# Attention: the row maxima are turned by VectorE in four blocks, the sign sits in the keys' constant row

## The chip, the cores and the metric

One core of a Trainium2 chip runs the whole program. The time is the device time of one execution in microseconds (us), and the number reported is the median of several runs. The core has five engines that run side by side, each through its own queue of instructions in order: TensorE (PE in the profile, with its weight loads as PEld), VectorE (DVE), ScalarE (ACT), GpSimd (POOL) and SyncE (SP, which here only issues transfers). They meet through semaphores.

## The reference

Four layers work on one sequence of 2048 tokens with 512 channels, all in fp32. Layers A are linear attention with learned features; layers B split the sequence into 4 segments of 512 tokens, and each segment is attended with a softmax, beside a memory of the segments before it. Only layer B's softmax matters here:

```python
for s in range(N):                       # 4 segments, 32 heads of 16 channels
    qs, ks, vs = q[:, :, s], k[:, :, s], v[:, :, s]
    logits = jnp.einsum("bhqd,bhkd->bhqk", qs, ks) * scale + mask
    p = _softmax(logits, axis=-1)
    a_dot = jnp.einsum("bhqk,bhkd->bhqd", p, vs)
    ...
x = x + _A_ref(...); x = x + _B_ref(...); x = x + _A_ref(...); x = x + _B_ref(...)
```

A softmax needs the maximum of each row of logits, so that the exponentials stay in range.

## The kernel before

A layer B works in quarter-steps, called m in the code: 8 of them in a segment (4 groups of 8 heads, each in two halves of 4 heads), 32 in a layer, 64 in the run. A quarter-step has five steps (R = 5), numbered k; the loop in `steps` (L1449) goes through k and issues, in program order, what belongs to each step. A table (`FIRST`, `GAPS`, `LAST`, `FINAL`) tells which further work is issued at which step: "2.0 m0 max turn t1 fin ln" is the first step of quarter-step 2. The wrapper `Ordered` (L144) and `held` (L164) tie every engine's instructions to the order in which the program issues them, so nothing moves on its own.

Each quarter-step holds queries and keys of its heads in the tiles Q and K, on 128 partitions: two groups of 64 rows. Of each group, 63 rows hold high and low parts of the values, and constants; row 63 (and 127) holds a constant 1 in K and is free in Q.

- `maxima(m)` runs 9 steps ahead of the attention (`LEAD`). It multiplies 63 rows of Q and K on TensorE, tokens on partitions, into two PSUM banks (tags "mx" and "my", or "g" in two of the five steps), and VectorE adds the mask and takes the maximum of each row in one instruction (L1165). Its accumulator goes to one column of the tile mxs, 128 tokens x 16 columns, one column for each of 4 heads and 4 blocks of 128 queries. The profile shows these instructions as CUSTOM_DVE_ANT_0, each with a DVE_READ_ACCUMULATOR2_ANT that writes mxs.
- `put_maxima(m)` (the word "max" in the table) comes in the step of the last of them. The maxima lie along partitions and are needed along a row, so TensorE turns mxs into the bank "mx" (L180, a transpose against the identity), ScalarE copies it to the tile mt with the factor -1, and at the next step the ScalarE queue issues a transfer from mt into rows 63 and 127 of Q (the list `self.later`).
- `attend(m)` begins four steps later. It multiplies all 64 rows, so that row 63 adds the negative maximum (Q) times 1 (K) to each logit. ScalarE exponentiates (P<-lg in the profile), GpSimd zeroes what lies above the diagonal, and `weighted(m)` multiplies by the values (g<-P,v) one step after the last block.

In the step in which `put_maxima` runs, the program's order is: products of the attention and of the maxima, then transfers and parts put off from earlier steps, then the weighted sums of the quarter-step before, and then the words of the table. There "m0" to "m3" (the memory's update, tile mem) stand ahead of "max", and "turn" (ot or tmp, through oh and ol), "a" (reading the memory: g<-mem,tb and r) and "fin" (turning U, then r and wt or ot) behind it.

The constants come from the host: column 25 of bd is 1 at partitions 15 and 31, and `constants` (L211) spreads it to the tile `ones`, from which `start` (L994) fills the constant rows of K. The tile mxs is taken anew for each quarter-step (two buffers), and so is mt.

Of the kernel before, what the change touches and what calls it, by code (L numbers as in the profile page):

```python
# [7 lines left out]
F32 = mybir.dt.float32  # L8
F32R = mybir.dt.float32r
BF16 = mybir.dt.bfloat16  # L10
AF = mybir.ActivationFunctionType
# [7 lines left out]
P = 128  # L19
# [11 lines left out]
MT = 2  # L31
# [69 lines left out]
def interleave_kernel(ctx, tc, x_in, a_wqkv, a_wphi, a_wo, b_wq, b_wk, b_wv, b_wo, b_beta,  # L101
# [13 lines left out]
    def nm(s):  # L115
        uid[0] += 1
        return f"{s}_{uid[0]}"

    def T2(tag, bufs, dt=F32, shape=(P, 512)):
        return sp.tile(list(shape), dt, tag=tag, bufs=bufs, name=nm(tag))  # L120

    def PS(tag, bufs, shape=(P, 512)):
        return ps.tile(list(shape), F32, tag=tag, bufs=bufs, name=nm(tag))
# [38 lines left out]
    dve, act, pool, sync = [Ordered(e) for e in (nc.vector, nc.scalar, nc.gpsimd, nc.sync)]  # L162

    def held(i):  # L164

        if last[0] is not None:
            behind(i, last[0])
        last[0] = i
        return i
# [3 lines left out]
    def mm(*a, **k):  # L173
        n = a[0].free_size()
        work[0] += n / 2.26 if k["rhs"].dtype == F32R else (n * 2 / 2.4 + 25 if "tile_position" in k else 2 * max(112, n * 2 / 2.4))
        return held(nc.tensor.matmul(*a, **k))  # L176

    def tp(*a):
        work[0] += 108
        return held(nc.tensor.transpose(*a))  # L180

    def dma(out, in_):
        sync.dma_start(out=out.bitcast(F32), in_=in_.bitcast(F32))

    ident = cp.tile([P, P], F32, name="ident")
    bd = cp.tile([P, 27], F32, name="bd")
# [793 lines left out]
    class LayerB:  # L980
# [6 lines left out]
        def start(self):  # L987
            mem = sp.tile([P, NC, 10 * VW], F32, tag="acc", bufs=1, name=nm("mem"))
            self.acc, self.kn = mem[:, :, 0 : 2 * VW], mem[:, :, 2 * VW :]
            self.sets = []  # L990
            for b in range(NSET):
                Q, K = [T2("e8", 2 * NSET, F32R, (P, 4, 512)) for _ in range(2)]
                self.sets.append((Q, K))
                for t, rows in ((Q, mask[0:32, 0:P]), (K, ones)):  # L994
                    dma(t[3:P:4].rearrange("p a t -> p (a t)"), rows.unsqueeze(1).broadcast_to([32, 16, P]))
                    yield
# [150 lines left out]
        def maxima(self, m):  # L1147


            s, c, hf = m // 8, m % 8 // 2, m % 2  # L1150
            Q, K = [t[:, 2 * hf : 2 * hf + 2, :] for t in self.st[s, c]["set"]]
            mx = T2("mxs", 2, shape=(P, 16))

            def prod(pb, r, i, at, w):
                for e in range(2):
                    q, k = Q[64 * e : 64 * e + 63, r, :], K[64 * e : 64 * e + 63, r, :]
                    mm(pb[e][:, at : at + w], lhsT=q[:, i * P : (i + 1) * P], rhs=k[:, 0:w],
                       start=True, stop=True, tile_position=(64 * e, 0))

            def top(pb, e, r, i, at):  # L1160
                n = (i + 1) * P
                col = (e * 2 + r) * 4 + i
                pl = pb[e][:, at : at + n]
                with tc.high_priority():
                    dve.tensor_tensor_reduce(  # L1165
                        out=pl, in0=pl, in1=mask[:, 512 - n : 512], scale=1.0, scalar=-3.0e38,
                        op0=ADD, op1=MAX, accum_out=mx[:, col : col + 1])

            for what in ([(0, 0, 0), (0, 2, P)], [(0, 3, 0)], [(1, 0, 0), (1, 2, P)],
                         [(0, 1, 0), (1, 1, 256)], [(1, 3, 0)]):  # L1170
                if self.k % R in SPARE if self.k >= 0 else self.k % 2:
                    pb = [PS("g", G) for _ in range(2)]
                else:
                    pb = [PS(t, 1) for t in ("mx", "my")]
                for r, i, at in what:
                    prod(pb, r, i, at, max(256, (i + 1) * P))
                for r, i, at in what:
                    for e in range(2):
                        top(pb, e, r, i, at)
                self.mx[m] = mx  # L1180
                yield

        def put_maxima(self, m):
            s, c, hf = m // 8, m % 8 // 2, m % 2
            Q = self.st[s, c]["set"][0][:, 2 * hf : 2 * hf + 2, :]
            pt = PS("mx", 1)
            tp(pt[0:16, 0:P], self.mx.pop(m), ident)
            mt = T2("mt", MT, F32R, shape=(16, P))
            act.activation(mt, pt[0:16, 0:P], AF.Copy, scale=-1.0)
            self.later.append(lambda: act.dma_start(out=Q[63:P:64].bitcast(F32), in_=mt.bitcast(F32)))  # L1190

        def attend(self, m):

# [366 lines left out]
```

## Time and profile before

| | us |
|---|---|
| median of 3 runs | 1357.32 |
| lowest and highest run | 1356.66, 1358.54 |
| span of the profiled execution | 1355.4 |
| attention of the first layer B, span's start at 0 | some 262 to 672 |
| attention of the second layer B | some 930 to 1330 |
| TensorE and VectorE busy in 850 to 990 (layer A's second pass, mostly) | 137.10 and 109.65 of 140.00 |

The profiled execution's span, from the first to the last instruction of the program, is its own time as far as the profile tells it. In a group of the page the busy time and the mean ns of one instruction stand behind the count, and then the idle time of the engine before them with what ended it. A row of the timeline gives start and duration, the engine, line and operation, the tiles written and read, the count of merged instructions, and in square brackets the idle time ahead of it with its releaser. A row of the waits gives who waited for whom, us in total, how many times and the longest. Most instructions show L154, the line of the wrapper, or L176 and L180, the helpers for matmuls and transposes, so the tiles' names tell them apart. The DMA of mt shows as e<-mt, as Q is a tile with the tag e8.

### The profile page before, as it was taken

Reading aid. Unit: us, or ns where it says so; the run is one execution under the profiler, and the core shown is the slowest. Engines: PE = TensorE matmul, PEld = TensorE weight load, DVE = VectorE, ACT = ScalarE, POOL = GpSimd, SP = SyncE. Lnnn points to the kernel's source line nnn. Section 1 sums busy time; section 2 is a strip of 40 time slices with the busy share of each in tenths; the row PEclk is TensorE's granted clock in tenths of the full one; section 3 lists DMA queues with packets and bytes.
Section 4 is the critical chain, followed back from the end, with each engine's and each line's share of the span. In section 5 each row is a group of like instructions: output and inputs, shape, how many; then the busy total and the mean of one; then the engine's idle time right before and its main releaser. Section 6 shows DMA issues by size and latency. Waiting matters only on the chain.

```text
span 1355.4 us, 36817 instructions
## 1 busy us (share of the span) xinstructions
PE 1315.4 (97%) x14056; PEld 1032.6 (76%) x14056; DVE 1039.5 (77%) x3256; ACT 808.6 (60%) x1205; POOL 695.8 (51%) x1060
## 2 busy tenths in 40 slices
PE   7999989999999999999999998999999999999998
PEld 6888868777777777877768886886777777777765
DVE  4766778777888888888667677787778879878883
ACT  5556345547677677677544433453667866766754
POOL 1668666326447557345324356553355656554442
PEclk9999999999999999999999999999999999999999
DMA  6398447535654545546250103755556554554431
GB/s 205 102 336 276 151 135 234 170 100 138 174 166 131 158 118 134 154 119 184 90 184 33 64 33 126 241 164 134 138 159 175 145 160 105 140 136 103 118 96 63
DMA packets 134401, 196.27 MB, mean 145 GB/s; under 512 B 15441, under 2 KB 61649, under 8 KB 133457
## 3 DMA queue, kind: packets, MB, share of 16 engines
q1 hardware_dynamic: 132256, 193.27, 48.9%
q8 instruction: 112, 1.84, 0.5%
q10 hardware_dynamic: 1968, 0.64, 0.2%
q14 instruction: 65, 0.52, 0.1%
HBM read 101.05 MB, written 39.85 MB: 104 GB/s over the span
## 4 chain that ended last, share of the span: by engine, by line
PE 74%; DVE 10%; ACT 5%; issue 4%; POOL 3%; DMA 3%; SPq 1%; ACTq 0%; DVEq 0%; POOLq 0%
PE g L176 56%; PE lg L176 6%; PE g L180 6%; PE mx L176 3%; ACT P L154 3%; POOL P L154 2%; DVE g L154 2%; PE lg L180 2%; SPq L154 1%; POOL tb L154 1%; PE my L176 1%; DMA x<-x 1%; DVE es L154 1%; PE mx L180 1%; DVE my L154 1%
## 5 line engine op out<-in xcount | busy, mean ns | idle before, releaser
L154 ACT ACTIVATE P<-lg 128x1024 f32<-128x1024 f32 x316 | 325.4, 1030 | 167.1 <-PE lg L176 92.5
L154 POOL TENSOR_SCALAR_AFFINE_SELECT P<-P 128x256 f32<-128x256 f32 (+1 forms) x448 | 193.4, 446 | 283.7 <-ACT P L154 279.1
L154 DVE CUSTOM_DVE_ANT_0 g<-g,mask 128x256 f32<-128x256 f32 (+3 forms) x392 | 191.3, 542 | 8.9 <-PE g L176 8.5
L176 PE MATMUL g<-hh,wqk 64*128 64x512 f32 (+1 forms) x960 | 187.3, 392 | 0.5 <-DMA wqk<-wqk 0.4
L176 PE MATMUL g<-w,oh 64*128 64x512 f32 (+2 forms) x880 | 178.9, 385 | 0.6 <-DVE ol L154 0.6
L154 DVE CUSTOM_DVE_ANT_0 mx<-mx,mask 128x512 f32<-128x512 f32 (+2 forms) x316 | 157.4, 498 | 21.5 <-PE my L176 13.7
L154 DVE CUSTOM_DVE_ANT_0 my<-my,mask 128x512 f32<-128x512 f32 (+2 forms) x316 | 163.3, 517 | 0.0
L176 PE MATMUL g<-P,v 128*32 128x128 f32 (+3 forms) x2064 | 151.6, 433 | 3.6 <-DVE mxs L154 2.5
L176 PE MATMUL lg<-e,e 64*128 64x512 f32 (+1 forms) x1010 | 152.0, 339 | 3.1 <-ACT P L154 3.1
L176 PE MATMUL g<-w,hh 64*128 64x512 f32 (+1 forms) x672 | 143.4, 395 | 2.0 <-ACT w L154 1.3
L154 DVE DVE_READ_ACCUMULATOR2_ANT mxs<- 128x1 f32 x1024 | 142.7, 139 | 0.0
L176 PEld LDWEIGHTS g<-P,v 128*32 128x32 f32 x2064 | 61.5, 109 | 87.3 <-issue 59.2
L176 PEld LDWEIGHTS lg<-e,e 64*128 64x128 f32 x1010 | 102.1, 185 | 32.3 <-issue 11.3
L176 PEld LDWEIGHTS g<-w,oh 64*128 64x128 f32 (+1 forms) x880 | 108.3, 186 | 15.6 <-issue 1.5
L176 PEld LDWEIGHTS g<-hh,wqk 64*128 64x128 f32 (+1 forms) x960 | 106.9, 185 | 16.4 <-PE my L176 1.2
L176 PE MATMUL g<-w,ol 64*128 64x512 f32 (+2 forms) x440 | 116.9, 378 | 0.5 <-DVE ol L154 0.5
L154 POOL TENSOR_SCALAR tb<-tb 128x512 f32<-128x512 f32 x72 | 109.0, 1526 | 16.0 <-ACT tb L154 16.0
L176 PE MATMUL g<-hl,wqk 64*128 64x512 f32 (+1 forms) x480 | 106.8, 390 | 0.2
L154 ACT COPY tb<-g 128x512 f32<-128x512 f32 (+1 forms) x132 | 71.1, 576 | 43.5 <-PE g L176 41.7
L176 PEld LDWEIGHTS g<-w,hh 64*128 64x128 f32 (+1 forms) x672 | 84.4, 188 | 16.1 <-ACT w L154 1.6
L176 PE MATMUL g<-w,hl 64*128 64x512 f32 (+1 forms) x336 | 90.2, 393 | 0.0
L154 DVE TENSOR_REDUCE es<-P 128x64 f32<-128x1024 f32 x64 | 77.3, 1208 | 12.8 <-ACT P L154 12.8
(151 smaller groups left out, 2896.9 us busy)
## 6 DMA issues: line engine op xcount, KB each, us to landing
e<-ta SPq DMA_DIRECT2D x384, 128.0 KB
wqk<-wqk SPq DMA_DIRECT2D x128, 256.0 KB
x<-x SPq DMA_DIRECT2D x48, 256.0 KB
ot<-in SPq DMA_DIRECT2D x26, 256.0 KB
pq<-tb SPq DMA_DIRECT2D x24, 256.0 KB
tb<-pq SPq DMA_DIRECT2D x24, 256.0 KB
x<-xr SPq DMA_DIRECT2D x22, 256.0 KB
xr<-x SPq DMA_DIRECT2D x20, 256.0 KB
```

Of the source, the lines that this page charges most:

```text
L154: i = f(*a, **k)
L176: return held(nc.tensor.matmul(*a, **k))
L180: return held(nc.tensor.transpose(*a))
```

## The change

The tile of the maxima gets 32 columns instead of 16, and is no longer taken anew: `start` takes two for the layer, fills them with zeros once on GpSimd, and the quarter-steps use them in turn. `put_maxima` turns them on VectorE: four transposes of 32 x 32 elements, each from 32 partitions of mxs into 32 columns of mt, which now has 32 partitions. The first 16 rows of mt are what the transfer takes; the other 16 hold the turned zeros. TensorE's transpose, the use of bank "mx" for it and ScalarE's copy go away. The maxima stay positive and unrounded in Q, and the constant row of K is -1.

```diff
@@ start
             self.sets = []
+            self.tops = [T2("mxs", 2, shape=(P, 32)) for _ in range(2)]
+            for t in self.tops:
+                pool.memset(t, 0.0)
@@ maxima
-            mx = T2("mxs", 2, shape=(P, 16))
+            mx = self.tops[m % 2]
@@ put_maxima
-            pt = PS("mx", 1)
-            tp(pt[0:16, 0:P], self.mx.pop(m), ident)
-            mt = T2("mt", MT, F32R, shape=(16, P))
-            act.activation(mt, pt[0:16, 0:P], AF.Copy, scale=-1.0)
-            self.later.append(lambda: act.dma_start(out=Q[63:P:64].bitcast(F32), in_=mt.bitcast(F32)))
+            mt, mx = T2("mt", MT, shape=(32, P)), self.mx.pop(m)
+            for b in range(4):
+                dve.transpose(out=mt[:, 32 * b : 32 * b + 32], in_=mx[32 * b : 32 * b + 32, :])
+            self.later.append(lambda: act.dma_start(out=Q[63:P:64].bitcast(F32), in_=mt[0:16]))
@@ kernel
-    bd[[15, 31], 25] = 1.0
+    bd[[15, 31], 25] = -1.0
```

## The prediction

> **What bounds the kernel now.** I read the page first, then the busy time of each engine in the two attention stages (columns: stretch, then busy time and instructions of PE, PEld, DVE, ACT, POOL, then clock and DMA).
>
> ```profile
> span 1355.4 us, 36817 instructions
> ...
> PE 1315.4 (97%) x14056; PEld 1032.6 (76%) x14056; DVE 1039.5 (77%) x3256; ACT 808.6 (60%) x1205; POOL 695.8 (51%) x1060
> ...
> PE 74%; DVE 10%; ACT 5%; issue 4%; POOL 3%; DMA 3%; SPq 1%; ACTq 0%; DVEq 0%; POOLq 0%
> PE g L176 56%; PE lg L176 6%; PE g L180 6%; PE mx L176 3%; ACT P L154 3%; POOL P L154 2%; DVE g L154 2%; PE lg L180 2%; SPq L154 1%; POOL tb L154 1%; PE my L176 1%; DMA x<-x 1%; DVE es L154 1%; PE mx L180 1%; DVE my L154 1%
> ```
> ```profile
> 262.00:672.00 410.00, 404.53 (x4377) 313.77 (x4375) 336.97 (x1286) 277.02 (x402) 205.59 (x362) 1.00 0.52 141
> 930.00:1330.00 400.00, 391.70 (x4347) 301.38 (x4348) 327.11 (x1259) 266.17 (x385) 205.11 (x356) 1.00 0.49 131
> ```
> TensorE is busy 796 of the 810 us in which the 64 quarter-steps of attention (32 in each of two layers, some 12.7 us each) run, with the granted clock at 1.00. So time is gained here only by taking work or idle time from TensorE, and lost by making it wait. VectorE is the next in line: 664 of 810 us, 82%. ScalarE (67%) and GpSimd (51%) have room.
>
> **The change, part by part.** *Removed: 64 TensorE transposes and 64 ScalarE copies.* Two views by tile carry them (columns: count, then shortest/median/longest ns), with the accumulator reads that fill the maxima:
>
> ```profile
> L154 DVE DVE_READ_ACCUMULATOR2_ANT mxs<- x1024: 132/140/145, 262.0 to 1322.5; 128x1 f32 x171
> ...
> L180 PE MATMUL mx<-ident,mxs x64: 276/277/278, 280.8 to 1323.4; 128*16 128x128 f32 x64
> ```
> ```profile
> L154 ACT ACTIVATE mt<-mx x64: 245/249/267, 281.1 to 1324.1; 16x128 fp32r<-16x128 f32 x64
> ```
> 64 x 277 ns would be 17.7 us, but matmuls overlap. Two places of the timeline tell what one transpose really takes: the first has it between the weighted sums (g<-P,v) and the four turns of ot, the second has the same neighbours without it.
>
> ```profile
> 614.00 2.36 PE L176 MATMUL g<-P,v 128*32 128x512 f32 x32
> 616.29 0.28 PE L180 MATMUL mx<-ident,mxs 128*16 128x128 f32 x1
> 616.40 0.60 PE L180 MATMUL g<-ident,ot 128*128 128x128 f32 x4
> ...
> 677.92 2.36 PE L176 MATMUL g<-P,v 128*32 128x512 f32 x32
> 680.21 0.66 PE L180 MATMUL g<-ident,ot 128*128 128x128 f32 x4
> ```
> With it, the sums end at 616.36 and the turns at 617.00: 0.64 us. Without it, 680.28 to 680.87: 0.59 us. The transpose is worth only 0.05 to 0.06 us (I take 0.057), since whichever matmul follows the narrow 128*32 ones pays for the changeover. The chain of waits books 1% (some 13 us) on it, because it charges it with that changeover; I do not believe that share.
>
> In some places even that is lost, because TensorE then waits for something the change does not move:
>
> ```profile
> 604.18 0.28 PE L180 MATMUL mx<-ident,mxs 128*16 128x128 f32 x1
> 604.29 0.60 PE L180 MATMUL g<-ident,ot 128*128 128x128 f32 x4
> 605.06 0.66 PE L180 MATMUL g<-ident,U 128*128 128x128 f32 x4 [0.16 <-ACT U L154]
> ```
> ```profile
> PE g L176 <- DVE mxs L154: 3.5, 11, 0.5
> ...
> PE g L180 <- ACT U L154: 2.5, 7, 0.6
> ```
> U is made from the weighted sums, so it comes no earlier. I count 13 such places (6 of these 7 waits that follow a transpose, and 7 where the memory product next in line waits for a VectorE result). That leaves 49 x 0.057 = 2.8 us, with the first step of each layer counted apart.
>
> The first step of each layer is dearer: there the next products need bank mx, and wait for the copy out of it.
>
> ```profile
> 280.84 0.22 PE mx L180
> 281.06 0.02 issue
> 281.08 0.28 ACT mt L154
> 281.36 0.04 issue
> 281.40 0.50 PE mx L176
> ```
> This is the chain itself: 1.06 us from 280.84 to 281.90. With the transpose gone the products follow at once, for some 0.4 us (an estimate: their 0.50, partly under the matmul before): 0.65 us saved, twice, 1.3 us. The bank is then free since VectorE's last reading of it, so VectorE is late next there, not ScalarE.
>
> The copies were on ScalarE, off the chain but for these two; 16 us less there I cost at nothing, as ScalarE's next work mostly waits for TensorE.
>
> *Added: 256 transposes on VectorE.* The trace has none. Nearest rows, all of 32 columns or fewer:
>
> ```profile
> L154 DVE RECIPROCAL rr<-es 128x32 f32<-128x32 f32 x32 | 11.3, 353 | 1.4
> ...
> L154 DVE TENSOR_TENSOR rr<-rr,es 128x32 f32<-128x32 f32 x32 | 6.2, 192 | 1.1
> ...
> L154 DVE TENSOR_SCALAR eb<-eb 128x32 f32<-128x32 f32 x1 | 0.2, 169 | 0.0
> ```
> The accumulator read (139 ns) is the floor, the reciprocal (353 ns) the ceiling; the one with one input and plain arithmetic (169 ns) is nearest. Four in a row, with 0.1 us for the wait on the maxima just written: between 4 x (0.139 - 0.08) + 0.1 = 0.34 us, if each overlaps the one before by 0.08 us as VectorE's neighbours do below (464.23 + 0.69 against 464.84), and 4 x 0.353 + 0.1 = 1.5 us without overlap. I take 0.75 us, by the 169 ns row hardly overlapped (0.78 without any overlap): 48 us on VectorE in all, 664 becoming 712 of 810 us (88%).
>
> [...]
>
> What hides the group is a hole: VectorE has nothing to do while TensorE runs the weighted sums. The tightest kind (with the memory update, mem, ahead of it) and a wide one:
>
> ```profile
> 464.23 0.69 DVE L154 SCALAR_TENSOR_TENSOR tb<-tb,tb 128x512 f32<-128x512 f32 x1
> 464.84 0.18 DVE L154 TENSOR_TENSOR mem<-g,mem 128x34 f32<-128x34 f32 x1
> 465.44 0.17 DVE L154 TENSOR_SCALAR r<-g 128x16 f32<-128x16 f32 x1 [0.42 <-PE g L176]
> ```
> ```profile
> 603.26 0.14 DVE L154 DVE_READ_ACCUMULATOR2_ANT mxs<- 128x1 f32 x1
> ...
> 605.65 0.69 DVE L154 TENSOR_TENSOR ol<-g,oh 128x512 fp32r<-128x512 f32 x1 [2.25 <-ACT oh L154]
> ```
> Laid out for all 60 steps behind the first two of each layer, the hole at the new instructions' place is 0.41 to 0.46 us in 10 steps, 0.64 in one, 0.82 to 1.05 in 21 and 1.5 to 2.7 in 28. At 0.75 us the overhang is 0.3 us in the 10 and 0.1 in the one: 3.2 us of VectorE lateness in all. At 0.9 us it is 5.0, at 1.2 us 12.4 (all 32 shorter holes), at 1.5 us 22. Queued behind the overhang are r and the next tops, which free TensorE's banks. Most of it is made good at the next hole some 2 us on, and TensorE's waits on the tops are 3.5 us in the whole run (first row of the waits above); I charge a third, 1.0 us. In the second group of tight steps (478 to 489 us) VectorE has no further hole before the next sums, so there it can cost in full.
>
> *Moved: the wait of the DMA that stores the turned maxima.* It stays one step later on ScalarE's queue, but waits for VectorE now. Behind it on that queue are the exponentials. The tightest step:
>
> ```profile
> 363.22 0.18 DVE L154 COPY mem<-g 128x34 f32<-128x34 f32 x1
> ...
> 364.89 0.52 ACTq L154 DMA_DIRECT2D e<-mt  x1
> ```
> From 363.40 to 364.89 are 1.49 us, twice the group; nothing is added up to there. SyncE's queue is not passed. The two zero fills per layer go to GpSimd ahead of the stage.
>
> ```profile
> L154 POOL MEMSET v<- 128x120 f32 x16 | 4.2, 259 | 0.0
> ```
> Four of at most 259 ns are 1.0 us of GpSimd in all; I cost them at nothing, as GpSimd is idle half of the time, and at 1.0 us if its queue is full just there. The sign in the constant row changes values alone. The copy also rounded; the DMA now takes unrounded words of the same size.
>
> **Sum:** -2.8 - 1.3 + 1.0 = -3.1 us; half a microsecond more for casts behind the removed copy (oh, hh), which start sooner by up to the copy's 0.25 us and give VectorE's next run an earlier start: **-3.6 us**. The profiled execution has 1355.4 us, 1.9 below the median of three, 1357.3, from which I carry it: **1353.7 us**.
>
> **The rivals.** *VectorE becomes the bound (slower).* Place: the 32 steps with holes of 1.05 us or less. For it: VectorE at 82% already, and four dependent small operations. Against: the 169 ns row. It decides where the overhang meets the gain: a group of about 0.9 us, if every overhang reaches TensorE. At 1.2 us it is 12.4 against 4.6 us gained: 1357.3 + 7.8 = 1365 us; above 1.49 us the DMA's wait holds up the exponentials too. [...]
>
> *Nothing is gained.* TensorE comes 0.057 us sooner to a wait that is already there: the sums wait for GpSimd's masks.
>
> ```profile
> PEld g L176 <- POOL P L154: 24.0, 56, 0.9
> ```
> For it: 56 such waits of weight loads, one in nearly every step. Against: the masks hang on products that come sooner as well. Then only the two first steps count, less some overhang: -0.8 us, 1356.5 us.
>
> *The chain is right.* If all of the 0.21 us by which the transpose ends behind the sums (616.36 to 616.57) goes each time, 64 x 0.21 = 13 us: 1344 us. The pair of timelines speaks against it.
>
> *The change does not do what it says:* the wait for VectorE lands on ScalarE instead. That needs more than 1.49 us and is the end of the first rival.
>
> **How the numbers follow.** The forecast (1351 to 1356 us) has 0.55, VectorE's bound 0.15, nothing gained 0.22, the whole chain share 0.08. A measurement can tell about 0.2%, 2.7 us, from no change. Of the forecast, 0.42 lies below 1354.6; with the last rival faster has 0.50. The rest of the forecast and nothing gained make 0.35 the same. VectorE's bound makes 0.15 slower. The range 1349 to 1359.5 leaves out most of the last rival and the dear half of VectorE's: some 0.17.
>
> **What would show it.** Right: L180 mx rows gone, TensorE's busy time in the stages down by 3 to 4 us, the four transposes under 0.2 us each and standing in the holes, ScalarE's queue not waiting for VectorE, first product at 281 us without its wait. Wrong: waits of "PE g" or "PE mx" on VectorE well above 3.5 us; holes at the tight steps gone and the sums starting late; a group over 0.9 us; or a P that waits behind the DMA.

## The result, and the profile after

The changed kernel takes 1365.24 us (median; 1364.28 to 1366.02), against 1357.31 us of the kernel before in the same comparison (1356.66 to 1358.54): ratio 1.0052 [1.004, 1.0065]. It is slower by some 7.9 us by the medians (7.1 by the ratio), where 3.6 us less were forecast, and outside the range of 1349 to 1359.5. The profiled execution had a span of 1362.6 us, 7.2 more than before.

The page of the changed kernel (busy time, share of the span, count):

```profile
span 1362.6 us, 36889 instructions
...
PE 1314.6 (96%) x13992; PEld 1030.9 (76%) x13992; DVE 1086.5 (80%) x3512; ACT 799.2 (59%) x1141; POOL 695.8 (51%) x1064
...
PE 73%; DVE 12%; ACT 4%; issue 3%; DMA 3%; POOL 2%; SPq 2%; ACTq 0%; DVEq 0%; POOLq 0%
```
The 64 transposes are gone from TensorE, the 64 copies from ScalarE (1205 to 1141), and VectorE has 256 instructions more. TensorE is busy for 0.8 us less, in a longer span. So it waits longer. The windows of the two attention stages (second one 10 us longer than the one shown of before) and the groups by line say that the new work costs what was expected of it:

```profile
262.00:672.00 410.00, 402.26 (x4334) 310.71 (x4336) 360.32 (x1410) 270.35 (x368) 205.68 (x365) 1.00 0.52 142
930.00:1340.00 410.00, 398.50 (x4368) 305.94 (x4368) 354.54 (x1398) 268.54 (x364) 206.07 (x359) 1.00 0.49 131
```
```profile
L154 DVE STREAM_TRANSPOSE mt<-mxs 32x32 f32<-32x32 f32 x256 | 50.9, 199 | 3.5
...
L154 POOL MEMSET mxs<- 128x32 f32 x4 | 0.4, 124 | 0.0
```
VectorE is busy for 714.9 of 820 us, 87%. One transpose takes 199 ns. TensorE's waits, from the view of the waits (who waited for whom: us, times, longest), first of the changed kernel, then the rows of before that the prediction doesn't show (mxs stands for the tops, VectorE's instructions that take the maxima):

```profile
PE g L176 <- ACT P L154: 11.5, 10, 2.7
...
PE g L176 <- DVE mxs L154: 4.2, 13, 0.6
PE my L176 <- issue: 4.2, 2, 3.3
```
```profile
PE g L176 <- ACT P L154: 6.6, 8, 1.1
...
PE my L176 <- issue: 3.1, 2, 1.9
```
The waits on the tops grew by 0.7 us only. The wait on ScalarE's P grew by 4.9 us with two waits more, one in each layer. That is the place of the loss.

Where it went in time is seen by matching every TensorE instruction of one trace with its like in the other, and taking the difference of their starts (called the offset below). That is worked out from the two traces, in us; the second column is the same change profiled once more (after2):

| stretch of the kernel before | after | after2 |
|---|---|---|
| start to 280.5 us | +2.0 | +0.6 |
| first quarter-step of layer 1, 280.5 to 290 | **+2.0** | **+4.8** |
| the rest of layer 1's attention and on to 829 | +0.7 | -0.2 |
| around 835 (a wait with no releaser) | +1.8 | +2.1 |
| 836 to 937 | -1.0 | -0.2 |
| first quarter-step of layer 2, 937 to 960 | **+1.4** | **+2.9** |
| the rest, to 1340 | +0.3 | +1.2 |

The first row differs by chance: in some executions, of other kernels below too, 16 of TensorE's products lg<-phibd take 3.8 us instead of 2.5 (3.79 in after and 3.78 in count, 2.46 in before and bearly; after2, the same program as after, is only 0.6 us later there). The two bold rows are in both profiles of the change. This is the place in layer 1, on the timeline (start, duration, what; in brackets the idle time ahead and its releaser), before:

```profile
281.38 1.19 ACTq L154 DMA_DIRECT2D e<-mt  x1
...
281.78 0.25 DVE L154 RECIPROCAL r<-g 128x16 f32<-128x16 f32 x1
...
282.93 2.34 PE L176 MATMUL g<-KN,P 128*64 128x68 f32 x64
283.03 1.01 ACT L154 COPY P<-lg 128x1024 f32<-128x1024 f32 x1 [1.68 <-PE lg L180]
```
and after:

```profile
283.17 1.09 PE L180 MATMUL lg<-ident,P 128*128 128x128 f32 x8
283.75 0.14 DVE L154 DVE_READ_ACCUMULATOR2_ANT mxs<- 128x1 f32 x1
...
284.19 1.17 PE L176 MATMUL g<-KN,P 128*64 128x68 f32 x32
284.66 0.43 DVE L154 TENSOR_TENSOR ot<-g,r 128x256 f32<-128x256 f32 x1
285.00 0.83 DVE L154 STREAM_TRANSPOSE mt<-mxs 32x32 f32<-32x32 f32 x4
285.86 1.13 ACTq L154 DMA_DIRECT2D e<-mt  x1
287.03 1.01 ACT L154 COPY P<-lg 128x1024 f32<-128x1024 f32 x1 [4.71 <-DVE mxs L154]
288.10 1.17 PE L176 MATMUL g<-KN,P 128*64 128x68 f32 x32 [2.74 <-ACT P L154]
```
Read it from below. TensorE waits 2.74 us for P. P is a ScalarE copy out of lg, which TensorE had finished by 284.26, but the copy starts only at 287.03: ScalarE's queue goes in order, and ahead of the copy stands the transfer of the turned maxima. That waits for the transposes, and they come at 285.00, because VectorE still has tops up to 283.89 and two pairs of r and ot up to 285.09 ahead of them. The backlog was there before as well: VectorE came to the first r at 281.78, when the transfer had already been issued, because TensorE and ScalarE turned the maxima without asking that queue. Layer 2 has the same gap, of 2.13 us:

```profile
952.88 1.17 PE L176 MATMUL g<-KN,P 128*64 128x68 f32 x32 [2.13 <-ACT P L154]
```

### The profile page after: what moved, and what is told of

Same layout as the page of the kernel before. It is cut to its first block, busy times and chain, and to the rows that moved or that the text cites. A ratio compares the mean times of both kernels' runs of the same rounds, so it can differ in the third digit from the quotient of the medians.

```text
span 1362.6 us, 36889 instructions
## 1 busy us (share of the span) xinstructions
PE 1314.6 (96%) x13992; PEld 1030.9 (76%) x13992; DVE 1086.5 (80%) x3512; ACT 799.2 (59%) x1141; POOL 695.8 (51%) x1064
## 4 chain that ended last, share of the span: by engine, by line
PE 73%; DVE 12%; ACT 4%; issue 3%; DMA 3%; POOL 2%; SPq 2%; ACTq 0%; DVEq 0%; POOLq 0%
PE g L176 56%; PE lg L176 6%; PE g L180 6%; PE mx L176 3%; ACT P L154 2%; DVE g L154 2%; SPq L154 2%; PE lg L180 1%; PE my L176 1%; DVE my L154 1%; DVE mx L154 1%; DVE mxs L154 1%; DMA x<-x 1%; DVE es L154 1%; ACT U L154 1%
```

## The experiments

**Which part of the change.** Four kernels. *null* keeps everything of the change (sign in the constant row, tiles kept and filled with zeros, the transfer from mt[0:16]) but the turning:

```diff
-            for b in range(4):
-                dve.transpose(out=mt[:, 32 * b : 32 * b + 32], in_=mx[32 * b : 32 * b + 32, :])
+            pt = PS("mx", 1)
+            tp(pt[0:16, 0:P], mx[:, 0:16], ident)
+            act.activation(mt[0:16], pt[0:16, 0:P], AF.Copy)
```


> All of the change but the transposes: the sign sits in the keys, the tile of the maxima is kept and filled with zeros, but TensorE still turns every quarter-step and ScalarE copies (factor 1). Theory 1 (the first quarter-step of each layer: its transfer holds up ScalarE's queue behind VectorE's backlog, some 2 to 2.7 us per layer): 1357 us, as before. Theory 2 (VectorE's load in the steps with short holes): 1357 us. Theory 3 (what the profile shows away from the transposes, +1.9 us in the first 25 us and +1.4 us in a TensorE wait without a visible cause near 835 us, comes with the changed program): between 1357 and 1360.6 us, and the profile shows slow products at 11 to 14 us again.

Measured: 0.9998 [0.9988, 1.0009]. The rest of the change costs nothing.

*hybrid* does the same for m = 0 of each layer only; the other 62 stay with VectorE (`if m > 0` ahead of the loop over b).

> As the change, but the first quarter-step of each layer (m = 0) is turned by TensorE and copied by ScalarE as before; the other 62 by VectorE. Theory 1: the loss at the two first steps goes, 2.0 to 2.7 us each, so 1360 to 1361 us from 1365.2. Theory 2: 62 of 64 groups stay on VectorE, so 1365 us. Theory 3: 1365 us.

Measured: 1.0007 [0.9993, 1.0021]. At 280 to 290 and at 937 to 960 us its offset doesn't change (0.14 to 0.13, 0.75 to 0.76). Almost the whole loss is gone with two of 64 groups given back.

*early* keeps VectorE for all, but asks for the first maxima four steps k sooner:

```diff
-          ... "k1/2", -11: "v2", -9: "max0"}
+          ... "k1/2", -13: "max0", -11: "v2"}
```


> As the change, but the first quarter-step's maxima are turned four steps sooner (k = -13 instead of -9), where VectorE has a hole of some 2.3 us, and their transfer is issued at k = -12. Theory 1: as the run before or a little better, since ScalarE's queue is free there and bank mx needs no copy (0.65 us per layer): 1359 to 1361 us. Theory 2: 1365 us. Theory 3: 1365 us.

Measured: 1.0018 [1.0005, 1.0032]. On its timeline the group stands ahead of VectorE's backlog, and the copy and the products follow without a gap:

```profile
276.79 0.84 DVE L154 STREAM_TRANSPOSE mt<-mxs 32x32 f32<-32x32 f32 x4
277.66 1.12 ACTq L154 DMA_DIRECT2D e<-mt  x1
...
284.25 2.34 PE L176 MATMUL g<-KN,P 128*64 128x68 f32 x64
...
284.35 1.01 ACT L154 COPY P<-lg 128x1024 f32<-128x1024 f32 x1 [2.23 <-PE lg L180]
```
Where an expectation below has the first maxima turned four quarter-steps sooner, four of these steps k are meant; a quarter-step has five. Of the 0.45 us that early gains at 281 us nothing stays: at 287 TensorE waits 0.42 us for VectorE's tmp.

*none* leaves the turning out altogether and transfers a tile of zeros, so the maxima are not subtracted.

> Leaves out the turning: the transfer takes a tile of zeros, so the maxima are computed but not subtracted (no TensorE transpose, no ScalarE copy, no VectorE transpose). It prices the removal alone. By the prediction's terms -4.1 us (2.8 and 1.3): 1353.2 us. If the changeover share of the chain of waits goes with each transpose, -13 us: 1344 us. Theory 3: 1353.2 plus 1.9 to 3.3 us.

Measured: 0.9985 [0.9975, 0.9995], 2.0 us less where 4.1 were expected. By this run that is all there is to win by the removal. From none to hybrid are 0.0022 or 3.0 us, with the two intervals some 2 us either way. They differ by VectorE's 62 groups, and by the two first transposes, which hybrid leaves to TensorE and none leaves out: these are worth 0.7 us each by the offsets (none goes from 2.23 to 1.53 at 281 us and from 1.54 to 0.84 at 943, hybrid stays as it was). So some 1.6 us are left for VectorE's groups.

**Is the first quarter-step enough by itself, and what would a longer group do?** *first* is hybrid turned round: VectorE only for m = 0, TensorE for the other 62 (`if m == 0`).

> The reverse of the mixed kernel: only the first quarter-step of each layer is turned by VectorE, the other 62 by TensorE and ScalarE. Theory 1: nearly the whole loss is here: 1.003 of before (+2.0 to 2.7 us twice, and TensorE's wait near 835 us still 1.9 us, as its program is two instructions shorter in front of it). Theory 2 (short holes): 1.000.

Measured: 1.0058 [1.004, 1.0077]; *after2*, the change once more beside it:

> The changed kernel again, for a second profile and a second time. If the +1.9 us at the start (TensorE's products at 214 ns instead of 112 ns until about 14 us instead of 11 us) is chance of one execution, this profile may have it or not, and the ratio lies a little below 1.0052. If it belongs to the program, it is here again. The hold-up at the two first steps (2.0 us or more each) and a TensorE wait of some 3.3 us near 839 us are there again by every theory.

Measured: 1.0057 [1.0036, 1.0079]. By the medians two groups make the loss of all 64. In its trace the two first quarter-steps cost 3.6 and 1.4 us; the rest of its 11.6 us lies elsewhere, 2.1 of it already in the first 25 us.

*double* makes each group of four transposes twice.

> As the change, with each group of four transposes made twice (the second writes the same again): 51 us more on VectorE. Theory 2 and the prediction's table of holes: at 1.7 us for a group the overhang in the 32 shorter holes is some 28 us, of which a part, a third to all, becomes time: 9 to 28 us more than the change, 1.012 to 1.026 of before. If VectorE's lateness is made good at later holes, the change costs only the doubled hold-up at the first steps: some 2 us more than the change, 1.007.

Measured: 1.0205 [1.0184, 1.0227]. Behind the first quarter-steps its offset grows by 9.9 us in layer 1 (290 to 672) and 8.8 in layer 2 (960 to 1340). The holes are full there: at 1.81 us a group (its 64 groups have 102.1 us of transposes and 15.0 us of idle time ahead of these) does delay TensorE, at 0.83 it hardly does.

**Is it ScalarE's queue, or the maxima coming late?** *spq* is the change with the first transfer on SyncE's queue:

```diff
-            self.later.append(lambda: act.dma_start(...))
+            self.later.append(lambda: (act if m else sync).dma_start(...))
```


> The change, with the transfer of each layer's first turned maxima (m=0 alone) issued by SyncE in place of ScalarE. VectorE's backlog stays, so the transposes are made at about 285.0 as in the change and the row lands near 288.1 (285.86 plus the 2.2 us that lie between the issue at 951.26 and the first use at 953.98 at most). Theory A (what costs is ScalarE's in-order queue alone: the copy P<-lg is stuck behind the transfer): the copy starts near 284.3, the gap of 2.74 us before g<-KN,P is gone and the time falls to early's 1.0013 to 1.0018. Theory B (the maxima themselves come too late): the gap moves to the products lg<-e,e of the first attention step, which wait for the row until about 288.1 in place of 285.9 + 0.5; of the 2.7 us about 1.1 are gained in each layer, so 1.7 us of the 7.9: 1.004 to 1.0055, less 0.002 more where the granted clock stays full because the gap is shorter.

Measured: 1.0042 [1.0027, 1.0058]. The copy is free, as theory A has it, and the gap is only moved, as theory B has it:

```profile
282.74 1.01 ACT L154 COPY P<-lg 128x1024 f32<-128x1024 f32 x1 [1.97 <-PE lg L180]
283.44 0.83 DVE L154 STREAM_TRANSPOSE mt<-mxs 32x32 f32<-32x32 f32 x4
284.30 0.64 SPq L154 DMA_DIRECT2D e<-mt  x1
...
286.22 0.49 PE L176 MATMUL lg<-e,e 64*128 64x512 f32 x2 [1.24 <-DMA e<-mt]
...
290.90 0.35 PE L176 MATMUL mx<-e,e 63*128 63x256 f32 x1 [0.82 <-DMA e<-ta]
```
The first attention products wait 1.24 us for the row itself, and 0.82 more go later, to a load that stood behind the transfer on SyncE's queue. In all, 1.7 and 1.8 us are lost there in the two layers. So VectorE's backlog is the cause, and ScalarE's queue only the place where it was felt.

**Can before gain by the earlier place?** *bearly* is the kernel before with "max0" moved as in early.

> The kernel before with one thing altered: the first maxima of each layer are turned (by TensorE and the ScalarE copy, as before) four quarter-steps sooner, behind the maxima's own products of that step rather than beside the side work at 281. In before the product mx<-e,e at 281.40 waits 0.35 us for the copy mt there; in the change this went (a gain of 0.7 at 282). If that gain can be had without the change, 0.35 to 0.7 us in each layer: 0.9990 to 0.9995. Rival: the same wait comes at the new place, where VectorE's maxima have only just been made: 0.9998 to 1.0003. It is the one candidate for a version faster than both.

Measured: 1.0088 [1.0071, 1.0105], a clear miss. At the new place the maxima are not yet made, and now it is TensorE's queue that stands still:

```profile
270.54 0.68 DVE L154 TENSOR_TENSOR ta<-tb,ta 128x512 fp32r<-128x512 f32 x1
271.14 1.21 DVE L154 TENSOR_REDUCE es<-P 128x64 f32<-128x1024 f32 x1
...
274.40 0.38 PE L180 MATMUL mx<-ident,mxs 128*16 128x128 f32 x1 [4.26 <-DVE mxs L154]
```
Each layer loses some 5 us there (offset -0.63 to 4.73 and 6.42 to 11.45). The same place is free in early, since there VectorE waits for nobody but itself. No version tried beats the kernel before but the one that leaves the turning out.

**The wait near 835 us.** In the product my<-v,P, behind layer 1's attention, TensorE stands still with nothing that releases it ("issue"). It is there before, too, but sits and lasts otherwise. Before, and in early:

```profile
830.25 0.99 PE L176 MATMUL my<-v,P 128*32 128x17 f32 x95
833.18 0.45 PE L176 MATMUL my<-v,P 128*32 128x17 f32 x33 [1.95 <-issue]
```
```profile
833.62 1.25 PE L176 MATMUL my<-v,P 128*32 128x17 f32 x127
838.57 0.20 PE L176 MATMUL my<-v,P 128*32 128x17 f32 x1 [3.69 <-issue]
```
It stands 32 products later where layer 1 has 32 transposes fewer (hybrid, with 31 fewer, has it after 126 products, first, with one fewer, after 96), so it seems to come at a fixed count of instructions. *pad* was to test that with empty instructions on TensorE in early, two in each quarter-step.

> The run with the earlier first turn, and two empty instructions on TensorE in each quarter-step, in the place of the weight load and the matmul that are gone (64 x 2), so that TensorE's program is as long as before. Theory 3 in its sharper form: the wait without a visible cause at the half of the products my<-v,P stands at a fixed number of instructions, 32 matmuls later when 32 are missing, and lasts 3.1 to 3.7 us there instead of 1.9 (before and null against all runs without the transposes). Then it is back at 1.9 us here, 1.2 to 1.8 us gained against the run without padding, less what 128 empty instructions cost: about 1.001 of before. If the wait has to do with other things, it stays at 3 us or more: 1.002.

Measured: 1.0013 [0.9999, 1.0027]. The empty instructions don't show in the trace: its page has 36889 instructions and 13992 products, as early's has, and the wait stands after product 127 as there. It is a second measurement of early, and says nothing on the count. *count* has real ones, at the start:

```diff
+    zero = cp.tile([P, 64], F32, name="zero")
+    pool.memset(zero, 0.0)
+    for _ in range(G):
+        pt = PS("g", G)
+        for i in range(8):
+            mm(pt[0:32, 32 * i : 32 * i + 17], lhsT=zero[:, 0:32], rhs=zero[:, 32:49], ...)
     run(p1[0], prepare())
```


> The version early (the change, but with the first maxima of each layer turned four quarter-steps sooner) with 32 extra matrix products of a tile of zeros on TensorE at the very start, where TensorE waits 4.9 us for its first load; nobody reads them, and they make up in number for the 32 transposes that layer 1 no longer issues on TensorE before 835 us. They take 32 products of about 10 ns in time that was idle. Theory 3 (the wait without a visible cause near 835 us comes at a fixed number of TensorE instructions from the start): the wait stands after product 95 of the 128 of my<-v,P again, as in the kernel before, and lasts about 1.9 us in place of 3.3 to 3.7, so the time is 1.4 to 1.8 us under early's 1.0013 to 1.0018, at 1.0000 to 1.0008. Rival a (the wait hangs on the place in the program or on the time, or the cost is not in this wait): it stays after product 127 with 3.3 us or more, and the ratio at 1.0013 to 1.0018. Rival b: the wait moves back to product 95 but keeps its length; then number and place go together and the cost does not.

Measured: 1.0019 [1.0008, 1.003]. The 32 calls became 64 products on TensorE:

```profile
0.99 3.60 PE L176 MATMUL g<-zero 128*32 128x17 f32 x64 [0.99 <-POOL zero L154]
```
```profile
833.05 0.72 PE L176 MATMUL my<-v,P 128*32 128x17 f32 x62
836.02 1.10 PE L176 MATMUL my<-v,P 128*32 128x17 f32 x66 [2.25 <-issue]
```
With 64 products more at the start the wait comes 65 products sooner, after 62 instead of 127, and lasts 2.25 us instead of 3.3 to 3.8. That it hangs on the count of TensorE's instructions is shown. That its length is what the time pays is not: count is no faster than early and pad (1.0019 against 1.0018 and 1.0013), though in its trace the place costs 0.2 us (offset 2.81 to 3.02 from 829 to 840 us), and in early's 1.8 (3.38 to 5.15).

The traces show what comes just before the wait ends. The page lists a DMA queue whose kind is "instruction", here before:

```profile
q8 instruction: 112, 1.84, 0.5%
```
The packed traces have the time of each of its 112 packets, of 16 KB. In all 13 profiles one of them ends 1.2 to 1.6 us before TensorE goes on (before at 831.78 and 833.18 us, early at 836.93 and 838.57, count at 834.65 and 836.02), and the shorter wait in the same product near 173 us, where a profile has it, ends in the same way. The author's reading is that TensorE waits there for the next piece of its program, at a place where it gets through 127 products in 1.25 us; no run tested this by itself.

## Why the prediction was wrong

**The step that failed** is "Moved: the wait of the DMA that stores the turned maxima", with its "From 363.40 to 364.89 are 1.49 us, twice the group; nothing is added up to there". That slack was read at one steady step, at 363 us, and the holes were laid out only for the 60 steps behind the first two of each layer. The first one, for which the prediction had just booked a gain, was not laid out for VectorE. There the slack is negative: the transfer of before went out at 281.38, and VectorE came to its r only at 281.78, with two pairs of r and ot still ahead of the transposes' place. The prediction even said that "VectorE is late next there", and didn't price it. ScalarE's copy of P came after the transfer, and TensorE waited 2.74 and 2.13 us for it in the two layers: the last of the prediction's own signs of being wrong, "a P that waits behind the DMA". By the table, -1.3 us became +2.0 and +1.4 in one execution, +4.8 and +2.9 in the other. hybrid, first and early show that this makes the change slow.

**The gain at 281 us** is real. In the change the products mx<-e,e follow the memory products at once (offset 1.97 to 1.26, so -0.7 us, forecast -0.65). It is lost again 2 us later.

**The granted clock** adds what the gap alone doesn't give. The windows of after2 (columns as in the prediction; the clock is third from the end):

```profile
283.00:287.00 4.00, 1.25 (x38) 1.11 (x36) 3.82 (x15) 1.01 (x1) 0.00 (x0) 0.88 0.20 43
287.00:291.00 4.00, 4.00 (x38) 3.14 (x35) 2.14 (x9) 1.02 (x1) 0.35 (x1) 0.50 0.00 0
291.00:295.00 4.00, 4.00 (x20) 3.03 (x20) 0.19 (x1) 0.91 (x2) 0.06 (x1) 0.77 0.02 4
```
and its products behind the gap, which take 1.17 us in the profile of after shown above:

```profile
286.70 2.08 PE L176 MATMUL g<-KN,P 128*64 128x68 f32 x32 [2.75 <-ACT P L154]
```
The gap is as long as in after (2.75 and 2.74 us), where the clock is 1.00 in every window from 275 to 300 us. In after2 it falls to 0.50, and the offset goes from 2.94 us at 284.5 to 5.41 at 290: some 2.5 us more. In 291 to 295 us the clock is 0.57 in first, behind a gap of 2.75 us, and 0.61 in double, behind one of 3.71 us, and in after2 it is 0.69 behind layer 2's gap (956 to 960). So the gap costs 2 us in one execution and nearly 5 in another, which is how the median can lie 7.9 us above before. A gap of 2.75 us was followed by a lower clock in two executions (after2 and first), and one of 2.74 us in a third (after) was not; what makes the difference no run shows.

**Removal.** The terms of 2.8 us, and 1.3 for the first steps, are measured together by none: 2.0 us (0.7 to 3.4 by its interval). The first steps are as forecast, 0.7 us each by the offsets, so the 2.8 us were too much; part of them goes to the wait near 835 us, which grows from 1.9 to 3.3 us where 32 transposes ahead of it are gone.

**The group** was priced at 0.75 us and takes 0.83 to 0.84, hardly anything of it being the wait on the maxima: 0.03 us, from 608.02 to 608.05, where the forecast had 0.1. A steady quarter-step of after:

```profile
607.88 0.14 DVE L154 DVE_READ_ACCUMULATOR2_ANT mxs<- 128x1 f32 x1
608.05 0.84 DVE L154 STREAM_TRANSPOSE mt<-mxs 32x32 f32<-32x32 f32 x4
610.13 0.69 DVE L154 TENSOR_TENSOR ol<-g,oh 128x512 fp32r<-128x512 f32 x1 [1.24 <-ACT oh L154]
```
It stands in the hole as forecast, with 1.24 us to spare. The four do not overlap (4 x 0.199 us and their small gaps make 0.84).

**Overhang.** 1.0 us was charged. In the traces the steady steps cost +0.7 to -0.2 us in layer 1 (removal and overhang together), with TensorE's waits on the tops 0.7 us longer. By the ratios, none against hybrid, VectorE's 62 groups cost some 1.6 us with some 2 either way, when the two first transposes are taken off. That fits what was charged, and doesn't settle it.

**The rivals.** "VectorE becomes the bound" had a time of 1365 us, and that is what came, but not by its mechanism: it named the 32 steps with short holes and a group of 1.2 us. double, at 1.81 us, shows that the steady steps do decide for longer groups. "The change does not do what it says: the wait for VectorE lands on ScalarE instead" is nearer to what happened, and was dismissed because it "needs more than 1.49 us", a slack of the wrong steps.

What stays open: why early, pad and count still lie at 1.0013 to 1.0019, without the gap of 2.7 us in their traces. By the offsets the rest of layer 1's attention (290 to 829 us) costs them 1.3 to 1.6 us, where after loses 0.7, after2 gains 0.2 and hybrid 1.0. VectorE's added work and the wait near 835 us are the candidates, and each is of that size.

## What to carry to other kernels

When work moves to another engine, lay out that engine's queue at every kind of place, and first of all in the ramp-up steps, where backlogs stand that the steady steps don't have; a slack found in the steady state says nothing of them. Here an instruction that waited on its queue delayed what was queued behind it, related or not: ScalarE's copy of P, whose input was ready at 284.26, started at 287.03, and TensorE stood for 2.74 us. Moving only the waiting transfer to another queue (spq) moved the gap (1.24 and 0.82 us in its place), and asking another engine's queue too soon (bearly) made a new one of 4.26 us, while giving the late engine the work earlier in its own queue (early) removed it. And an idle gap of the bounding engine can cost twice, in the gap and in the clock after it: in after2 2.75 us, and some 2.5 us more at a clock of 0.50.

## What the hardware showed that was not expected

- A TensorE gap of 2.75 us was followed by a granted clock of 0.50 and products of 2.08 us instead of 1.17 in one execution (after2), and by no change in another with a gap of 2.74 us (after, 1.00 and 1.17 us).
- TensorE stands still for 1.7 us (first) to 4.0 us (double) near 835 us at a place that moves with the number of its instructions: 32 transposes fewer, 32 products later; 64 products more, 65 sooner. In all 13 profiles a packet of the queue of kind "instruction" ends 1.2 to 1.6 us before it goes on.
- Empty instructions on TensorE (pad) left no instruction in the page's counts, and didn't move that place.
- One 128 x 16 fp32 transpose on TensorE, 277 ns by its row, is worth some 0.03 us of the time on the mean (none: 2.0 us for 64, with the copies gone too), and 0.7 us where the next products wait for its bank.
